# Turning two quarters of the second token group ahead of four products of the first, and pinning four small VectorE operations behind the turned copies

## The chip, the cores and the metric

The kernel runs on one core of a Trainium2 chip. The core has TensorE for matrix products (the profile shows its matmuls as PE and its weight loads as PEld), VectorE (DVE), ScalarE (ACT), GpSimd (POOL) and SyncE (SP), which here issues every DMA. The metric is the device time of one execution in microseconds (us).

## The reference

The input x has 2048 tokens of 448 channels. It is normalised per token (`xn`), and the result is x plus two branches of `xn`:

```python
xn = _layernorm(x, axis=-1)
return x + _A_ref(xn, A_w_r, A_w_i) + _B_ref(xn, B_w1, B_w2, B_w3, B_w4)
# A: real 2-D Fourier transform of xn, times w_r + 1j * w_i, transformed back
# B:
h  = _gelu(_layernorm(x) @ w1)                 # 448 x 448
hs = shifted(h) @ w2                           # each quarter of the channels shifted by +1, -1, +2, -2 tokens
x1 = x + hs
out = x1 + _gelu(_layernorm(x1) @ w3) @ w4     # 448 x 1792 and 1792 x 448
```

The change touches the first part of branch B alone: the product with w1.

## The kernel before

**Tiling.** The tokens lie on 128 partitions as 16 blocks of 128, and the blocks are worked on in four groups of four (`GRP`). Group 0 and group 1 are turned (channels brought to the partitions) on TensorE: `turn_pe(g, t)` writes quarter t of the channels (128 of them, 64 in the last) of all four blocks into one PSUM bank with four transposes (L428). `turn_copy` then makes a high f16 half on ScalarE (L438) and the low half that is left on VectorE (L439). Groups 2 and 3 are turned otherwise: `turn(g)` makes the two halves first (L940 to L942) and sends them block by block through a transposing DMA on SP's queue (L943) into `w4x`, which is the turned input of the products.

**The product with w1.** `w1_in` (L479) multiplies turned blocks with `w1p` in three passes (high by high, low by high, high by low), 44 matmuls of 448 columns for a group. Group 0's four accumulators are `first` (pw1_00 to pw1_03); group 1's are pw1_10 to pw1_13, group 2's pw1_20 to pw1_23. `w1_unit` takes one accumulator further: gelu on ScalarE (L500), a high half (L502) and a low half on VectorE (L503), and a transposing DMA on SP's queue into `h` (L506). The products with w2 (`w2_mm`, L524) read `h`.

**The spreads of the weights.** `powers` forms a power of two for a weight matrix: a sum over partitions by a product with ones (L258, `pm`), then three one-column VectorE operations in `factors`: L265 reads the bank, L267 gives the scale, L270 its inverse. For w2 these are `s2` and `r2`; L1043 to L1045 combine them with w1's into `s12`, which GpSimd reads first at L403.

**What sets the order.** The program is recorded in source order and put in order by a scheduler with its own notion of time; `behind(key)` tells it that what is inside has to stand behind a named instruction, and is no wait on the chip. A row of the orders below with `[waits ...]` waits for a semaphore: each engine counts on one of its own, and a DMA posts on one of eight (DMAHW0 to DMAHW7) taken in turn, after it has itself waited for that semaphore's last user. So the DMAHW name in the row of a DMA is the one that it will post on. Each engine, SP's queue too, works its instructions off strictly in the order in which they stand.

**PSUM banks.** Banks come from pools with two buffers for a name. `pm2`, the bank of the sum for w2, and the last two quarters of group 1 (pta12, pta13) share the two banks called "acc": pta13 takes the bank of `pm2` and has to wait until L265 has read it.

Of the kernel before, what the change touches and what calls it, by code (L numbers as in the profile page):

```python
# [16 lines left out]
ALU = mybir.AluOpType  # L17
# [13 lines left out]
EPS = 1e-5  # L31
# [91 lines left out]
def body(tc, nc, x, wf, w1, w2, w3, w4, c_g, c_n, c_small, out):  # L123
    V, A, P, T, SY = nc.vector, nc.scalar, nc.gpsimd, nc.tensor, nc.sync
# [28 lines left out]
    def bank(tag, name):  # L153
        return ps.tile([128, 512], F32, tag=tag, bufs=2, name=name)
# [10 lines left out]
    def xb(b):  # L165
        g, i = WHERE[b]
        return xt[g][:, i]
# [80 lines left out]
    def powers(m, n, key, tag="acc", mid=None, pin=None, down=0):  # L248

        t = pc.tile([128, 1], F32, name=f"pt{key}")  # L250
        i = V.tensor_reduce(out=t, in_=m[:, :n + 1], axis=AX.X, op=ALU.add)
        after["t" + key] = (i.ins,)
        if mid:
            with behind("t" + key):
                mid()
        pm = bank(tag, f"pm{key}") if isinstance(tag, str) else tag
        with behind(*pin) if pin else contextlib.nullcontext():
            i = T.matmul(pm[:, 0:1], ones, t, start=True, stop=True)  # L258
        after["p" + key] = (i.ins,)
        s, r = factors(pm, key, down)  # L260
        return s, r()

    def factors(pm, key, down=0):
        e = pc.tile([128, 3], I32, name=f"pe{key}")
        V.tensor_scalar(out=e[:, 0:1], in0=pm.bitcast(I32)[:, 0:1], scalar1=1, scalar2=0x7F800000,  # L265
                        op0=ALU.logical_shift_right, op1=ALU.bitwise_and)
        V.tensor_scalar(out=e[:, 1:2], in0=e[:, 0:1], scalar1=-1, scalar2=(185 - down) << 23, op0=ALU.mult, op1=ALU.add)  # L267

        def inverse():
            i = V.tensor_scalar(out=e[:, 2:3], in0=e[:, 0:1], scalar1=1, scalar2=(69 + down) << 23, op0=ALU.mult, op1=ALU.add)  # L270
            after["s" + key] = (i.ins,)
            return e.bitcast(F32)[:, 2:3]

        return e.bitcast(F32)[:, 1:2], inverse
# [61 lines left out]
    def stats1(g, ks):  # L336
        if g not in mvs:
            mvs[g] = pc.tile([128, 4, 2], F32, name=f"mva{GRP[g][0]}")
        stats([xb(GRP[g][k]) for k in ks], f"a{GRP[g][ks[0]]}", mvs[g][:, ks[0]:])
# [70 lines left out]
    after = {}  # L410

    @contextlib.contextmanager
    def behind(*key):
        key = key if len(key) > 1 else key[0]
        with contextlib.ExitStack() as st:
            for i in after[key]:
                st.enter_context(tc.issue_after(i))
            yield
# [4 lines left out]
    def turn_pe(g, t):  # L423
        pt = bank((("mm", "mm", "tr", "tr") if g == 2 else ("tr", "tr", "acc", "acc"))[t], f"pta{g}{t}")
        w = 128 if t < 3 else 64
        with behind("T", g) if ("T", g) in after else contextlib.nullcontext():
            for i, b in enumerate(GRP[g]):
                m = T.transpose(pt[:w, 128 * i:128 * i + 128], xb(b)[:, 128 * t:128 * t + w], ident)  # L428
        after["T", g] = (m.ins,)
        return pt[:w]  # L430
# [42 lines left out]
    def w1_in(g, units, ts, passes=range(3)):  # L473
        for p in passes:
            for t in ts:
                for i, pm in units:
                    wi, xi = ((0, 0), (0, 4), (4, 0))[p]
                    if t < 3 or p != 1:
                        m = T.matmul(pm[:, :D], xTs[g][:, xi + t, 128 * i:128 * i + 128], w1p[:, wi + t],  # L479
                                     start=t == 0 and p == 0, stop=t == 3 and p == 2)  # L480
        return m
# [507 lines left out]
    with behind("p1"):  # L989
        pts = [turn_pe(0, 0)]  # L990
    with behind("T", 0):
        norm_of([3])
    with behind("n", 0):
        s1, r1 = factors(pm, "1")
# [3 lines left out]
    first = [bank("mm" if k < 2 else "sp", f"pw1_0{k}") for k in range(4)]  # L998
# [9 lines left out]
    with behind("w1", -1):  # L1008
        r1 = r1()
    h1 = pc.tile([128, 1], F32, name="h1")  # L1010
# [10 lines left out]
    with behind("n", 1):  # L1021
        pts = [turn_pe(1, t) for t in range(2)]
        with behind("T", 1):
            s2, r2 = powers(m2, 1, "2", "acc", lambda: stats1(2, [0]))
        with behind("p2"):
            after["T", 1] = (w1_in(0, list(enumerate(first)), [3], [2]).ins,)
    with behind("np", 1):
        n1[0][1]()
    with behind("g", 0):
        n1[1][0]()  # L1030
        n1[1][1]()
    pts += [turn_pe(1, 2), turn_pe(1, 3)]
    for t in range(4):
        turn_copy(1, t, pts[t])
    with behind("g", 1):
# [4 lines left out]
        with behind("g", 1):  # L1040
            low()
    s12 = pc.tile([128, 4], F32, name="s12")
    V.tensor_tensor(out=s12[:, 0:1], in0=h1, in1=s2, op=ALU.mult)  # L1043
    V.scalar_tensor_tensor(out=s12[:, 1:2], in0=r1, scalar=2.0 ** 5, in1=r2, op0=ALU.mult, op1=ALU.mult)
    V.tensor_scalar(out=s12[:, 2:3], in0=s12[:, 0:1], scalar1=s12[:, 0:1], scalar2=EPS, op0=ALU.mult, op1=ALU.mult)  # L1045
    p12, eps12 = s12[:, 1:2], s12[:, 2:3]
    stats1(2, [1])
    with behind("a1"):
# [35 lines left out]
    for k in range(4):  # L1084
        n = 128 if k < 3 else 64
        with behind(*((1, 3), (1, 3), (1, 3), (2, 0))[k]):
            squares(m3[:n, k:k + 1], w3raw[:n, k])
    s3, r3 = powers(m3, 4, "3", "sp", pin=("u", 2, 3))
    h3 = pc.tile([128, 1], F32, name="h3")
    V.tensor_scalar(out=h3, in0=s3, scalar1=2.0 ** -6, scalar2=None, op0=ALU.mult)  # L1090
# [23 lines left out]
    for i in range(7):  # L1114
        with behind(3, 3):
            squares(m4[:, i:i + 1], flat(w4raw[:, 2 * i:2 * i + 2]), junk4)
    s4, r4 = powers(m4, 7, "4", down=1)
    p34 = pc.tile([128, 2], F32, name="p34")
    V.scalar_tensor_tensor(out=p34[:, 1:2], in0=r3, scalar=2.0 ** 6, in1=r4, op0=ALU.mult, op1=ALU.mult)
# [122 lines left out]
```

## Time and profile before

| | |
|---|---|
| median of 3 runs | 407.5 us (407.41 to 408.04) |
| the profiled execution, its own time | 407.2 us |
| span of its instructions | 405.4 us |
| TensorE matmul busy | 400.4 us, 99% of the span |
| VectorE, ScalarE, GpSimd busy | 304.4, 267.8, 170.1 us |
| mean granted TensorE clock | 1.0 |

The part that the change touches lies at 19 to 24 us of the span, what it moves farther down at 24 to 60 us; from 60 us on the program consists of the products with w3 and w4 and the Fourier branch. A row of the timeline gives start, length, engine, line, operation, output and inputs, the count of like instructions merged into it, and in brackets the idle time of the engine ahead of it and what ended it. SPq rows are DMAs as SP issues them: the length is that of the issue, not of the transfer.

### The profile page before, as it was taken

How to read it: one execution, taken by the hardware profiler on the slowest of the kernel's cores; microseconds unless marked ns; L12 is line 12 of the kernel's file. 1: busy time of each engine (PE TensorE's matmuls, PEld its weight loads, DVE VectorE, ACT ScalarE, POOL GpSimd, SP SyncE). 2: the span in 40 equal slices, each digit the busy share in tenths (PEclk: the TensorE clock that was granted, in tenths of full speed). 3: DMA queues.
4: the chain of work that ended last, by engine and by line, in shares of the span. 5: the costliest groups of instructions: out<-in, count | busy, mean ns of one | idle time of the engine just before them, and what ended most of it. 6: DMA issues, size and time to landing. Idle time of an engine off the chain costs nothing.

```text
span 405.4 us, 8824 instructions
## 1 busy us (share of the span) xinstructions
PE 400.4 (99%) x3383; PEld 296.6 (73%) x3383; DVE 304.4 (75%) x657; ACT 267.8 (66%) x464; POOL 170.1 (42%) x269
## 2 busy tenths in 40 slices
PE   8999999999999999999999999999999999999996
PEld 4554556666677877776878878877788888888885
DVE  6999999889545658883677777763588879889745
ACT  4699985874738766862687888785956566544332
POOL 2888911001397746599143434431231264211000
PEclk9999999999999999999999999999999999999999
DMA  8999999907910383417054556632000022233201
GB/s 283 340 285 191 175 176 254 267 2 153 211 48 1 100 280 123 115 36 176 15 154 124 144 153 163 156 92 60 1 2 2 24 68 74 89 111 103 84 2 45
DMA packets 57209, 49.46 MB, mean 122 GB/s; under 512 B 41312, under 2 KB 52192, under 8 KB 57168
## 3 DMA queue, kind: packets, MB, share of 16 engines
q1 hardware_dynamic: 57168, 48.91, 46.1%
q8 instruction: 26, 0.43, 0.5%
q14 instruction: 15, 0.12, 0.1%
HBM read 35.06 MB, written 3.67 MB: 96 GB/s over the span
## 4 chain that ended last, share of the span: by engine, by line
PE 99%; DVE 0%; issue 0%
PE pw L449 33%; PE acc L826 24%; PE pw L524 9%; PE pw L479 8%; PE cr L841 4%; PE acc L841 3%; PE pu L722 3%; PE ps L619 3%; PE pp L676 2%; PE pe L742 2%; PE px L693 2%; PE py L764 2%; PE wps L922 2%; PE pta L428 1%; PE end L826 1%; PE pm L985 0%
## 5 line engine op out<-in xcount | busy, mean ns | idle before, releaser
L449 PE MATMUL pw<-x2mem,w3p 128*128 128x256 f16 x1232 | 149.5, 272 | 0.0
L449 PEld LDWEIGHTS <-w3p 128*128 128x128 f16 x1232 | 118.8, 98 | 19.3
L826 PE MATMUL acc<-w4p,hf 128*128 128x448 f16 x508 | 107.3, 352 | 0.0
L826 PEld LDWEIGHTS <-hf 128*128 128x128 f16 x532 | 51.4, 98 | 35.7
L792 DVE SCALAR_TENSOR_TENSOR hf<-pw,h,hf 128x512 f16<-128x512 f32 x56 | 41.8, 747 | 36.0 <-ACT hf L791 35.8
L788 ACT ACTIVATE pw<-pw,pe 128x512 f32<-128x512 f32 x56 | 36.7, 656 | 43.9 <-PE pw L449 43.7
L791 ACT ACTIVATE hf<-pw,h 128x512 f16<-128x512 f32 x56 | 38.3, 683 | 1.2
L524 PE MATMUL pw<-w2p,h 112*128 112x448 f16 x192 | 39.0, 352 | 0.0
L749 POOL TENSOR_TENSOR e<-e 128x226 f32<-128x226 f32 x16 | 10.8, 674 | 64.2 <-ACT e L746 60.9
L479 PE MATMUL pw<-w1p,w4x 128*128 128x448 f16 x176 | 34.8, 352 | 0.5 <-DVE pe L270 0.5
L524 PEld LDWEIGHTS <-h 112*128 112x128 f16 x192 | 18.6, 98 | 16.0 <-DMA h<-x2mem 0.6
L703 POOL TENSOR_TENSOR xr<-te 128x450 f32<-128x450 f32 x16 | 15.7, 982 | 34.1 <-DVE te L701 34.1
L479 PEld LDWEIGHTS <-w4x 128*128 128x128 f16 x176 | 17.1, 98 | 16.4 <-ACT w4x L438 0.7
L711 POOL TENSOR_TENSOR zb<-xr,zb 128x450 f16<-128x450 f32 x16 | 16.2, 1010 | 17.1 <-ACT zb L710 16.5
L756 ACT ACTIVATE vh<-e 128x448 f16<-128x448 f32 x16 | 9.2, 576 | 15.6 <-DVE e L754 15.4
L699 DVE SCALAR_TENSOR_TENSOR te<-px,sc,wc 128x450 f32<-128x450 f32 x16 | 11.0, 686 | 10.3 <-ACT te L698 6.8
L698 ACT ACTIVATE te<-px 64x450 f32<-64x450 f32 x32 | 17.3, 540 | 1.7 <-PE px L693 1.2
L734 ACT ACTIVATE U<-y 113x512 f16<-113x512 f16 x32 | 18.0, 620 | 0.1
L746 ACT ACTIVATE e<-pe 128x452 f32<-128x452 f32 x16 | 8.7, 545 | 13.0 <-PE pe L742 10.1
L726 DVE SCALAR_TENSOR_TENSOR y<-pu,y 113x512 f16<-113x512 f32 x16 | 10.9, 688 | 6.9 <-ACT y L725 6.8
L757 DVE TENSOR_TENSOR vh<-e,vh 128x448 f16<-128x448 f32 x16 | 10.0, 624 | 7.1 <-ACT vh L756 7.1
L598 POOL TENSOR_TENSOR xr<-xf 128x452 f32<-128x452 f32 x6 | 6.7, 1125 | 20.2 <-issue 10.1
(205 smaller groups left out, 786.8 us busy)
## 6 DMA issues: line engine op xcount, KB each, us to landing
wc<-wf SPq DMA_DIRECT2D x32, 225.0 KB, 3.6
wl<-wf SPq DMA_DIRECT2D x8, 450.0 KB, 3.8
xt<-x SPq DMA_DIRECT2D x3, 896.0 KB, 11.6
w3raw<-w SPq DMA_DIRECT2D x3, 896.0 KB, 14.8
xf<-x SPq DMA_DIRECT2D x6, 448.0 KB, 3.7
xr<-x SPq DMA_DIRECT2D x12, 224.0 KB, 2.5
out<-xr SPq DMA_DIRECT2D x12, 224.0 KB, 2.0
gn<-c_g SPq DMA_DIRECT2D x16, 128.0 KB, 3.0
```

Of the source, the lines that this page charges most:

```text
L449: m = T.matmul(ps_out, wp[:, wi + t, cols], xT[:, xi + t, tok], start=t == 0 and wi + xi == 0, stop=t == 3 and wi == 4)
L479: m = T.matmul(pm[:, :D], xTs[g][:, xi + t, 128 * i:128 * i + 128], w1p[:, wi + t], start=t == 0 and p == 0, stop=t == 3 and p == 2)
L524: m = T.matmul(w2b[b][:, :D], hT[g][:112, 4 * hi + k, o:o + 128], w2p[:, wi, k], start=k == 2 and hi + wi == 0, stop=k == 3 and hi == 1)
L698: i = A.activation(out=e[64 * h:64 * h + 64], in_=px_[64 - 64 * h:128 - 64 * h, :2 * DF], func=AF.Copy)
L703: P.tensor_tensor(out=z, in0=t[:, 0], in1=t[:, 1], op=ALU.add)
L711: P.tensor_tensor(out=zv[1], in0=z, in1=zv[0], op=ALU.subtract)
L734: A.activation(out=U[b][:113, p].rearrange("p q (c k) -> p q c k", c=NC), in_=Y1[:113, p, :, :, b], func=AF.Copy)
L788: A.activation(out=pm, in_=pm, func=AF.Gelu_apprx_tanh, scale=r3)
L791: i = A.activation(out=h[:, 0], in_=pv_, func=AF.Copy, scale=h3)
L792: j = V.scalar_tensor_tensor(out=h[:, 1], in0=pv_, scalar=h3, in1=h[:, 0], op0=ALU.mult, op1=ALU.subtract)
L826: m = T.matmul(to, h[:, hi, 2 * f + i], w4p[0][:, wi, 2 * fp + f, r], start=fp == s and f == 0 and hi + wi == 0, stop=fp == e and f == 1 a ...
L841: m = T.matmul(to, h[:, hi, slot] if slot < 4 else g[:, hi, slot - 4], w4f[fp][k][wi], start=k in (0, 6) and fp == 0 and hi == 0, stop=hi ...
```

## The change

Two edits. The first: `turn_pe(1, 2)` and `turn_pe(1, 3)` are recorded where the four products that finish group 0 (quarter 3, third pass, one for each accumulator) were, and these four products behind them. The second: L270 for w2 (`r2`) and the three operations on `s12` are recorded behind the turned copies of group 1 (`behind("a1")`); `powers` returns `r2` uncalled for that.

```diff
-        return s, r()
+        return s, r() if key != "2" else r
...
         with behind("p2"):
-            after["T", 1] = (w1_in(0, list(enumerate(first)), [3], [2]).ins,)
+            pts += [turn_pe(1, t) for t in range(2, 4)]
...
-    pts += [turn_pe(1, 2), turn_pe(1, 3)]
+    with behind("T", 1):
+        w1_in(0, list(enumerate(first)), [3], [2])
     for t in range(4):
         turn_copy(1, t, pts[t])
...
     s12 = pc.tile([128, 4], F32, name="s12")
-    V.tensor_tensor(out=s12[:, 0:1], in0=h1, in1=s2, op=ALU.mult)
-    V.scalar_tensor_tensor(out=s12[:, 1:2], in0=r1, scalar=2.0 ** 5, in1=r2, op0=ALU.mult, op1=ALU.mult)
-    V.tensor_scalar(out=s12[:, 2:3], in0=s12[:, 0:1], scalar1=s12[:, 0:1], scalar2=EPS, op0=ALU.mult, op1=ALU.mult)
+    with behind("a1"):
+        r2 = r2()
+        V.tensor_tensor(out=s12[:, 0:1], in0=h1, in1=s2, op=ALU.mult)
+        V.scalar_tensor_tensor(out=s12[:, 1:2], in0=r1, scalar=2.0 ** 5, in1=r2, op0=ALU.mult, op1=ALU.mult)
+        V.tensor_scalar(out=s12[:, 2:3], in0=s12[:, 0:1], scalar1=s12[:, 0:1], scalar2=EPS, op0=ALU.mult, op1=ALU.mult)
```

The number of instructions on every engine stays the same, and so does every operand. Three places in the order matter.

On TensorE, behind the sum for w2 (pm_350 is `pm2`; pta_355 and pta_371 are quarter 2 of group 1 in the two builds, pta_360 and pta_376 quarter 3; + is the changed kernel):

```order
 L258 MATMUL pm_350<-pt_344,ones 128x1
+L428 MATMUL pta_355<-ident,xt_77 128x128 x4
+L428 MATMUL pta_360<-ident,xt_77 64x128 x4
 L479 LDWEIGHTS w4x
 L479 MATMUL pw_00_219<-w1p,w4x 128x448
@@ -139,6 +141,4 @@
 L479 LDWEIGHTS w4x
 L479 MATMUL pw_03_222<-w1p,w4x 128x448
-L428 MATMUL pta_371<-ident,xt_77 128x128 x4
-L428 MATMUL pta_376<-ident,xt_77 64x128 x4
 L479 LDWEIGHTS w4x
 L479 MATMUL pw_10_447<-w1p,w4x 128x448
```

The eight transposes went ahead of the four products; what stands behind both is group 1's first product, pw_10, as before.

On VectorE, the four low-half copies of group 1 (L439) and the small operations:

```order
 L267 TENSOR_SCALAR pe_352<-pe_352 128x1
+L439 TENSOR_TENSOR w4x<-pta_339,w4x 128x512
+L439 TENSOR_TENSOR w4x<-pta_355,w4x 128x512
+L439 TENSOR_TENSOR w4x<-pta_360,w4x 64x512
 L270 TENSOR_SCALAR pe_352<-pe_352 128x1
-L439 TENSOR_TENSOR w4x<-pta_339,w4x 128x512
-L1043 TENSOR_TENSOR s_397<-h_257,pe_352 128x1
-L1044 SCALAR_TENSOR_TENSOR s_397<-pe_208,pe_352 128x1
-L1045 TENSOR_SCALAR s_397<-s_397 128x1
-L439 TENSOR_TENSOR w4x<-pta_371,w4x 128x512
-L439 TENSOR_TENSOR w4x<-pta_376,w4x 64x512
+L1046 TENSOR_TENSOR s_396<-h_257,pe_352 128x1
```

The copies of quarters 1, 2 and 3 now follow each other, and the small operations stand behind them; L265 and L267 stay ahead.

On SP's queue, farther down, the four transposing DMAs that turn group 2 (L943, one for each of its blocks; the scheduler has moved these by itself):

```order
 L506 DMA_TRANSPOSE h_446<-hs_119 128x8x128 [waits DMAHW4_49,DVE_49]
 L943 DMA_TRANSPOSE w4x<-x_463 128x7x128 [waits DVE_49,DMAHW5_49,PE_49,Activation_49]
-L943 DMA_TRANSPOSE w4x<-x_463 128x7x128 [waits DMAHW6_49,PE_49]
+L943 DMA_TRANSPOSE w4x<-x_463 128x7x128 [waits DMAHW6_49,DVE_49,Activation_49]
 L943 DMA_TRANSPOSE w4x<-x_463 128x7x128 [waits DVE_49,DMAHW7_49,PE_49,Activation_49]
 L943 DMA_TRANSPOSE w4x<-x_463 128x7x128 [waits DMAHW0_49,PE_49]
```

The row of the first DMA reads the same in both builds, but it now carries block 1 of the group, and the second, which has got waits for its own data, carries block 0. What TensorE waits for shows it. Ahead of the first product of group 2 (pw_20, block 0) TensorE stood before:

```order
L524 MATMUL pw_1_532<-w2p,h_446 128x448
L524 LDWEIGHTS h_446
L524 MATMUL pw_1_532<-w2p,h_446 128x448
L479 LDWEIGHTS w4x [waits DMAHW5_49]
L479 MATMUL pw_20_631<-w1p,w4x 128x448 [waits DVE_49]
```

and in the changed kernel:

```order
L524 MATMUL pw_1_532<-w2p,h_446 128x448
L524 LDWEIGHTS h_446
L524 MATMUL pw_1_532<-w2p,h_446 128x448
L479 LDWEIGHTS w4x [waits DMAHW6_49]
L479 MATMUL pw_20_631<-w1p,w4x 128x448 [waits DVE_49]
```

The weight load of block 0 waited for the first of the four DMAs (DMAHW5), and now waits for the second (DMAHW6), while the place of the product in TensorE's order has not moved. Later on SP's queue the last L943 of group 3 and one L506 of group 2 have changed places as well.

## The prediction

> **What bounds the kernel now.** I read the page's busy times and its chain of waits first, then what TensorE waited for, then the timeline of the stretch that the change touches, and last the queue of SP behind it.
>
> ```profile
> PE 400.4 (99%) x3383; PEld 296.6 (73%) x3383; DVE 304.4 (75%) x657; ACT 267.8 (66%) x464; POOL 170.1 (42%) x269
> ...
> PE 99%; DVE 0%; issue 0%
> ```
>
> The whole chain that ends last is TensorE's own queue. What TensorE waited for, with total, times and longest:
>
> ```profile
> PE wps L922 <- DVE x2mem L188: 1.2, 1, 1.2
> PE pw L479 <- DVE pe L270: 0.5, 1, 0.5
> ```
>
> Both waits lie at the start, ahead of the change. So the kernel has no slack on TensorE: the change removes no matmul, hence it can gain only what small gaps TensorE still has behind 19 us, and any new wait of TensorE goes into the time in full. A matmul's record is longer than its step, so gaps below some 0.16 us do not show as idle time; I get them from counts. The timeline:
>
> ```profile
> 12.39 6.97 PE L479 MATMUL pw<-w1p,w4x 128*128 128x448 f16 x36
> ...
> 19.84 1.09 ACT L438 ACTIVATE w4x<-pta 128x512 f16<-128x512 f32 x2 [1.69 <-PE pta L428]
> ...
> 20.08 0.28 PE L258 MATMUL pm<-pt,ones 128*128 128x1 f32 x2
> ...
> 20.22 0.92 PE L479 MATMUL pw<-w1p,w4x 128*128 128x448 f16 x4
> ...
> 20.40 0.16 DVE L265 TENSOR_SCALAR pe<-pm 128x1 int32<-128x1 int32 x1 [0.73 <-PE pm L258]
> ...
> 20.98 1.04 PE L428 MATMUL pta<-ident,xt 128*128 128x128 f32 x8
> ...
> 21.20 0.68 DVE L439 TENSOR_TENSOR w4x<-pta,w4x 128x512 f16<-128x512 f32 x1
> ...
> 21.61 1.07 ACT L438 ACTIVATE w4x<-pta 128x512 f16<-128x512 f32 x2 [0.68 <-PE pta L428]
> ...
> 21.80 0.15 DVE L1043 TENSOR_TENSOR s<-h,pe 128x1 f32<-128x1 f32 x1
> ...
> 21.85 8.65 PE L479 MATMUL pw<-w1p,w4x 128*128 128x448 f16 x44
> ...
> 22.24 1.41 DVE L439 TENSOR_TENSOR w4x<-pta,w4x 128x512 f16<-128x512 f32 x2
> 22.58 0.59 ACT L500 ACTIVATE pw<-pw,gsc 128x448 f32<-128x448 f32 x1
> 23.21 0.63 ACT L502 ACTIVATE hs<-pw,h 128x448 f16<-128x448 f32 x1
> ...
> 23.70 6.36 PEld L479 LDWEIGHTS <-w4x 128*128 128x128 f16 x35 [0.43 <-DVE w4x L439]
> ...
> 23.87 0.68 DVE L503 SCALAR_TENSOR_TENSOR hs<-pw,h,hs 128x448 f16<-128x448 f32 x1 [0.23 <-ACT hs L502]
> ```
>
> The step of a 448-column product is (6.97 - 0.35) / 35 = 0.189 us (0.35 is one record). At 23.70 a weight load of group 1 waited for the copy of the last quarter, which ended at 22.24 + 1.41 = 23.65. How much of that reached the products:
>
> ```profile
> 30.34 7.09 PE L524 MATMUL pw<-w2p,h 112*128 112x448 f16 x36
> 37.27 7.92 PE L479 MATMUL pw<-w1p,w4x 128*128 128x448 f16 x41
> ```
>
> 44 products from 21.85 to 30.34 took 8.49 us where 44 x 0.189 is 8.32: a gap of 0.17. 36 products from 30.34 to 37.27 took 6.93 where 36 x 0.189 is 6.80: 0.13 more. These 0.3 us are all that the change can win between 19 and 37 us.
>
> **The front of the change.** The eight transposes start at 20.22 and not at 20.98, 0.76 earlier. They take 21.85 - 20.98 = 0.87, so the four products run from 21.09 and group 1 starts at 21.85 as before: the swap itself costs TensorE nothing. ScalarE's copy of quarter 2 was released at 21.61; it now could start at 20.85 but ScalarE copies quarters 0 and 1 until 19.84 + 1.09 = 20.93, so the gain is about 0.7, and gelu goes from 22.58 to about 21.85. VectorE lost 22.24 - 21.80 = 0.44 to the small operations between its copies; with these behind, quarters 1, 2 and 3 follow each other from 21.15 and end near 23.15 instead of 23.65. The weight load that waited at 23.70 wanted to go at 23.70 - 0.43 = 23.27, so the 0.17 goes.
>
> The bank of `pm2`: quarter 3's first transpose comes four steps of 0.11 (0.87 / 8) after 20.22, at 20.66, and needs L265, which ended at 20.56. That is 0.10 ahead, and holds, since L265 still stands ahead of the copies; if it failed the price would be under 0.1. Cost 0. `s12` ends later by about 1.2 us; it is read first here:
>
> ```profile
> 36.10 0.57 POOL L403 TENSOR_SCALAR cs<-cs,s 128x4 f32<-128x4 f32 x2
> ```
>
> With 13 us to spare these four operations cost nothing, and L270's result goes into `s12` alone.
>
> **What it triggers on SP's queue.** The first transposing DMA waits for L503 at 23.87, which now follows gelu and L502 0.75 earlier. So SP starts its chain at up to 24.64 - 0.75 = 23.89. Each row: start, length of the issue.
>
> ```profile
> 24.64 1.66 SPq L506 DMA_TRANSPOSE h<-hs  x1
> ...
> 26.41 1.96 SPq L506 DMA_TRANSPOSE h<-hs  x1
> ...
> 28.48 1.25 SPq L506 DMA_TRANSPOSE h<-hs  x1
> ...
> 29.83 2.65 SPq L506 DMA_TRANSPOSE h<-x2mem  x2
> 32.57 1.29 SPq L506 DMA_TRANSPOSE h<-hs  x1
> 34.03 5.29 SPq L943 DMA_TRANSPOSE w4x<-x  x4
> ...
> 35.34 1.25 SPq L943 DMA_TRANSPOSE w4x<-x  x1
> ```
>
> Each issue starts some 0.1 to 0.2 us behind the end of the one before: from 24.64 on SP itself is the limit, eight issues long, down to the second L943. And there TensorE stands close behind:
>
> ```profile
> 34.98 2.01 PEld L524 LDWEIGHTS <-h 112*128 112x128 f16 x12 [0.38 <-DMA h<-x2mem]
> 37.15 2.87 PEld L479 LDWEIGHTS <-w4x 128*128 128x128 f16 x16 [0.16 <-DMA w4x<-x]
> ```
>
> The time from issue to landing stands last in the row of a DMA:
>
> ```profile
> w4x<-x SPq DMA_TRANSPOSE x1, 3.1
> ```
>
> The first L943 (34.03, landing 3.1 later at 37.13) was block 0 of group 2, and the weight load at 37.15 took it at once; the product followed at 37.27. In the changed order block 0 rides in the second L943: issued at 35.34, 3.1 to land (its row reads the same), so 38.44 - x, where x is how much earlier SP's chain comes to that place. With the 0.02 to 0.05 from landing to weight load the product starts at 38.49 - x instead of 37.27: **TensorE ends up 1.22 - x later than before**. The 0.3 won ahead of it is in that already, since it only makes TensorE wait longer here.
>
> **How large x is.** Its ends are 0, if the earlier start is eaten up by longer issues, and 0.75, if every issue keeps its length. The two first issues are the long ones, 1.66 and 1.96 against 1.25 to 1.29, 1.1 us more in all. The stretches, with the DMA engines' share and GB/s last:
>
> ```profile
> 22.00:24.00 2.00, 2.00 (x12) 0.89 (x10) 1.70 (x5) 1.97 (x5) 2.00 (x5) 1.00 1.00 419
> 24.00:26.00 2.00, 2.00 (x13) 0.99 (x12) 1.82 (x4) 2.00 (x5) 1.92 (x4) 1.00 1.15 291
> 26.00:28.00 2.00, 2.00 (x12) 1.06 (x11) 1.79 (x5) 2.00 (x5) 1.79 (x2) 1.00 1.25 127
> ```
>
> Up to 24 us the engines are full with the loads of x and w3; when the transposes come in, the rate falls and the share stays above 1. A transpose issued 0.75 earlier meets 0.75 x 419 = 315 KB more of loads, and that has to be moved at the slow rate, with the issues stretched for longer. So x lies nearer to 0 than to 0.75; I take 0.3, and TensorE is 1.22 - 0.3 = 0.9 us late from 37 us on. That is an estimate from these rows. The first of them took this long to land, where the L943 took 3.1:
>
> ```profile
> h<-hs SPq DMA_TRANSPOSE x1, 5.3
> ```
>
> The Trainium skill, page "DMA: Bandwidth & Descriptors", section "Queues, rings and completion order", says that on each DMA engine descriptors are consumed in ring order; all of this kernel's DMAs stand in SP's row of rings, so by it alone the transposes cannot pass the loads, x would be close to 0 and the loss 1.2 us. The trace agrees in part, with 5.3 us against 3.1; it does not tell how much of the issue time goes with it.
>
> Nothing behind 37 us can give the loss back, since TensorE has no idle time there. The sum for the profiled execution: 407.2 + 0.9 = 408.1. The runs' median is 0.3 above that execution, so 407.5 + 0.9 = **408.4 us**.
>
> **The rivals.** *A second wait.* The other swap on SP's queue puts a transpose of `h` (group 2) behind the last L943 of group 3:
>
> ```profile
> 50.53 1.25 SPq L506 DMA_TRANSPOSE h<-x2mem  x1
> 51.94 1.22 SPq L943 DMA_TRANSPOSE w4x<-x  x1
> ...
> 54.25 0.48 PEld L524 LDWEIGHTS <-h 112*128 112x128 f16 x3
> ```
>
> and the landing of the first of these rows:
>
> ```profile
> h<-x2mem SPq DMA_TRANSPOSE x1, 3.2
> ```
>
> It would be issued at about 51.9, land 3.2 later at 55.1, and be wanted at 54.25 + 0.9 = 55.15. If SP's queue is late there by as much as TensorE, it costs up to 0.85 more: 409.2 us. Against it: the group 3 halves ahead of it on that queue don't wait for TensorE's late products, and the changed order puts two more products ahead of the one that wants it (0.4 us).
>
> *No wait at all, and the time not slower.* If the first two issues fall back to 1.25 because the loads are done with, x is 0.75 + 1.1 = 1.85, the second L943 lands at 36.6, ahead of 36.97 where TensorE would want it, and the 0.3 stays: 407.2 us. The point from which it decides is x = 1.22. The 419 GB/s of loads right before 24 us speak against it.
>
> *The full shift.* x = 0.75: 0.47 late, 408.0 us; this is the low end of my own case, as x = 0 (408.7) is its high end.
>
> *The change does nothing.* The swap of blocks 0 and 1 would have to be harmless because TensorE comes to group 2 later anyhow; but every product between 20 and 37 us stands where it stood, and only gaps have gone. 407.5 us.
>
> **How the numbers follow.** 0.2% of 407.5 is 0.8 us, about what a measurement of this kernel can tell from no change. My case (408.0 to 408.7) gets 0.76: 0.27 of it below 408.3, 0.49 above. The second wait gets 0.08, no wait, or a change that does nothing, 0.11, time lost at a place that I don't see 0.03, and won there 0.02. So slower by over 0.2%: 0.49 + 0.08 + 0.03 = 0.60; within 0.2%: 0.27 + 0.11 = 0.38; faster: 0.02. The range runs from 407.6, between no wait and the full shift, to 409.0, short of the second wait's end.
>
> **What the profile of the changed kernel would show.** TensorE's waits: a new line for L479 waiting for the DMA of `w4x`, 0.6 to 1.2 us, at 37 us, and the row of 41 products there starting near 38.2; no wait of a weight load for L439 at 23.7; gelu L500 near 21.9, and SP's first transpose near 23.9. If the first two issues are again 1.7 to 2.0 long and the third starts later than 27.7, x was eaten as I say. I am wrong if the second L943 is issued ahead of 34.1, if TensorE shows no wait at 37 us, or if its order lets it do other work there.

## The result and the profile after

The changed kernel takes 408.72 us (median of 15 runs, 407.83 to 409.71), the kernel before 407.5 us in the same comparison (407.28 to 408.41). The ratio is 1.002, with a 95% interval of 1.0011 to 1.0029: slower by 0.45 to 1.2 us. The profiled execution took 407.97 us with a span of 406.2 us, so it lies near the fast end of its own kernel; the median is 0.75 us longer.

The page of the changed kernel, busy times and chain:

```profile
PE 399.8 (98%) x3383; PEld 296.7 (73%) x3383; DVE 304.6 (75%) x657; ACT 268.0 (66%) x464; POOL 171.9 (42%) x269
...
PE 93%; DVE 3%; ACT 2%; DMA 1%; issue 0%; DVEq 0%; ACTq 0%
```

TensorE is busy for 0.6 us less (99% to 98%) in a span that is 0.8 us longer: it waits more. What TensorE waited for (total, times, longest):

```profile
PE wps L922 <- DVE x2mem L188: 1.2, 1, 1.2
PE pw L479 <- DVE xt L531: 0.8, 1, 0.8
PE pm L985 <- ACT xr L246: 0.6, 2, 0.3
PE pw L479 <- DVE pe L270: 0.5, 1, 0.5
```

The second row is new, and stands ahead of group 2's first product; the third is new too, but lies near 7 us, ahead of the change. The second names VectorE, since L531 happened to end at 38.01 in this execution, and the chain follows it there (DVE 3%, ACT 2%); the weight load of that product names a DMA instead, and so do the rows of the same wait in all later profiles. The timeline of the changed kernel, TensorE's queue and the copies:

```profile
21.21 9.24 PE L479 MATMUL pw<-w1p,w4x 128*128 128x448 f16 x48
21.22 2.00 DVE L439 TENSOR_TENSOR w4x<-pta,w4x 128x512 f16<-128x512 f32 x3
21.95 0.59 ACT L500 ACTIVATE pw<-pw,gsc 128x448 f32<-128x448 f32 x1
...
23.39 0.68 DVE L503 SCALAR_TENSOR_TENSOR hs<-pw,h,hs 128x448 f16<-128x448 f32 x1
...
30.29 6.97 PE L524 MATMUL pw<-w2p,h 112*128 112x448 f16 x36
...
38.02 2.00 PEld L479 LDWEIGHTS <-w4x 128*128 128x128 f16 x12 [1.19 <-DMA w4x<-x]
38.02 8.50 PE L479 MATMUL pw<-w1p,w4x 128*128 128x448 f16 x44 [0.75 <-DVE xt L531]
```

The 48 products from 21.21 run without a gap (the weight load's wait at 23.7 is gone), gelu begins at 21.95 instead of 22.58, and then group 2's first product starts at 38.02 instead of 37.27: 0.75 later. SP's queue in the same execution (start, length of the issue):

```profile
24.14 1.34 SPq L506 DMA_TRANSPOSE h<-hs  x1
...
25.64 2.23 SPq L506 DMA_TRANSPOSE h<-hs  x1
...
27.97 1.28 SPq L506 DMA_TRANSPOSE h<-hs  x1
...
33.54 1.24 SPq L943 DMA_TRANSPOSE w4x<-x  x1
```

The first transposing issue is 0.50 earlier, the second 0.77 (it is then held longer), and from the third down to the first L943 (34.03 before) everything is 0.5 earlier. Group 2's first product comes 38.02 - 33.54 = 4.48 behind that issue: one more issue and 3.1 us of landing.

### The profile page after: what moved, and what is told of

Same layout as the page of the kernel before. It is cut to its first block, busy times and chain, and to the rows that moved or that the text cites. A ratio compares the mean times of both kernels' runs of the same rounds, so it can differ in the third digit from the quotient of the medians.

```text
span 406.2 us, 8827 instructions
## 1 busy us (share of the span) xinstructions
PE 399.8 (98%) x3383; PEld 296.7 (73%) x3383; DVE 304.6 (75%) x657; ACT 268.0 (66%) x464; POOL 171.9 (42%) x269
## 4 chain that ended last, share of the span: by engine, by line
PE 93%; DVE 3%; ACT 2%; DMA 1%; issue 0%; DVEq 0%; ACTq 0%
PE pw L449 33%; PE acc L826 24%; PE pw L524 7%; PE pw L479 6%; PE cr L841 4%; PE acc L841 3%; PE pu L722 3%; PE ps L619 3%; PE pp L676 2%; PE pe L742 2%; PE px L693 2%; PE py L764 2%; DVE sta L326 1%; DMA xt<-x 1%; ACT pw L500 1%; PE pta L428 1%
## 5 line engine op out<-in xcount | busy, mean ns | idle before, releaser
L479 PE MATMUL pw<-w1p,w4x 128*128 128x448 f16 x176 | 34.4, 352 | 1.3 <-DVE xt L531 0.8
L479 PEld LDWEIGHTS <-w4x 128*128 128x128 f16 x176 | 17.1, 98 | 17.3 <-DMA w4x<-x 1.2
L711 POOL TENSOR_TENSOR zb<-xr,zb 128x450 f16<-128x450 f32 x16 | 16.1, 1009 | 17.1 <-ACT zb L710 16.5
```

The lines of the kernel that those rows point to most:

```text
L711: P.tensor_tensor(out=zv[1], in0=z, in1=zv[0], op=ALU.subtract)
```

## Experiments

Two times are used in all of them, both counted from the same instruction, the start of the pm matmul L258 near 20 us, so that what happens ahead of the change (19.89 to 20.70 us) drops out. The table is worked out from the rows of each timeline; the landing of the last w3 load is its issue (L219) plus the time from issue to landing in its row. "Product" is group 2's first L479 behind the 36 products of w2.

| kernel | L258 at | last w3 load lands at | third L506 issue at | first L943 issue, from L258 | product, from L258 |
|---|---|---|---|---|---|
| before | 20.08 | 28.62 | 28.48 | 13.95 | 17.19 |
| before, second profile | 20.46 | 29.65 | 29.59 | 14.69 | 18.07 |
| before, third profile | 20.01 | 28.09 | 28.46 | 14.02 | 17.35 |
| changed | 20.16 | 28.06 | 27.97 | 13.38 | 17.86 |
| changed, second profile | 20.22 | 29.12 | 29.04 | 14.38 | 18.84 |
| changed, third profile | 20.12 | 28.34 | 28.30 | 13.74 | 18.36 |
| changed, block 0 first | 20.35 | 28.26 | 28.25 | 13.44 | 16.94 |
| before, swap alone | 20.34 | 28.15 | 28.10 | 13.46 | 17.99 |
| before, turn alone | 20.70 | 28.65 | 28.66 | 13.53 | 18.11 |
| before, pinned alone | 19.89 | 28.20 | 28.16 | 13.83 | 17.19 |
| changed, both orders back | 20.10 | 28.80 | 28.74 | 14.18 | 17.55 |
| changed, no late loads | 19.94 | none | 26.78 | 12.95 | 17.45 |
| before, no late loads | 20.43 | none | 27.88 | 13.44 | 17.07 |

**Block 0 first.** The changed kernel; each L943 of group 2 is ordered behind the one of the block ahead of it:

```diff
-            d = SY.dma_start_transpose(out=xTs[g][:, :, 128 * i:128 * i + 128], in_=h)
+            with behind("td", g, i - 1) if g == 2 and i else contextlib.nullcontext():
+                d = SY.dma_start_transpose(out=xTs[g][:, :, 128 * i:128 * i + 128], in_=h)
+            after["td", g, i] = (d.ins,)
```

> The changed kernel, with the four L943 transposes of group 2 held in the order of their blocks, so that block 0 goes first again. Theory (the loss is block 0 riding in the second L943): the 0.75 us step of TensorE at 37 us and its weight load's 1.2 us wait are gone; the first L943 is issued near 33.5 and lands near 36.6, ahead of the 36.97 at which TensorE wants it, so the 0.3 us won ahead of it stay: 407.2 us, ratio to the kernel before 0.9993, and slower than before by nothing. Rival (the loss lies in the turned quarters or the small operations themselves): the step at 37 us goes but 0.5 us or more turn up elsewhere, 408 us or more, ratio above 1.001. Rival (second wait): as TensorE is on time again, the transpose of h that stands behind the last L943 of group 3 is now late at 54 us by 0.1 to 0.5 us: 407.3 to 407.7.

Measured: 408.17 us, ratio 1.001 (1.0001 to 1.0018). The step at 37 us is gone, the product comes 0.25 earlier than in the first profile of before; but at 54 us a new wait stands. TensorE in this kernel:

```profile
37.29 8.49 PE L479 MATMUL pw<-w1p,w4x 128*128 128x448 f16 x44
...
55.27 0.74 PE L524 MATMUL pw<-w2p,h 112*128 112x448 f16 x3 [0.27 <-DMA h<-x2mem]
```

From start to start the gap there is 0.43 above the step. So block 0's place is what costs time at 37 us, and the order holds a second loss in reserve, which shows only when TensorE is on time: 0.43 - 0.25 = 0.18 late in the profile, within the interval (0.04 to 0.73 us). The 407.2 of the theory failed. The second wait came as its rival said (0.1 to 0.5 us), but the median lies above that rival's 407.7 and inside the range of the other one (408 or more); the profiled execution is the fastest of its eleven. What speaks for the second wait is the trace, in which nothing else is lost behind the product (see the two kernels again, below).

**Swap alone.** The kernel before; block 1's L943 of group 2 goes ahead of block 0's, and nothing else is changed:

```diff
+            def send(i=i, h=h):
+                with behind("td", 2, 1) if g == 2 and i == 0 else contextlib.nullcontext():
+                    d = SY.dma_start_transpose(out=xTs[g][:, :, 128 * i:128 * i + 128], in_=h)
...
+        for i in (1, 0, 2, 3) if g == 2 else range(4):
+            d = sends[i]()
```

> The kernel before with one edit: block 1's L943 of group 2 is sent ahead of block 0's; nothing else of the change. Theory: SP's chain starts at 24.64 as before, so x is 0 and TensorE is 1.22 us late at 37 us: 408.7 us, ratio 1.0030, with a weight load of L479 waiting for the DMA of w4x there. Rival (the order of the two blocks doesn't matter, the loss is elsewhere): 407.5 us, ratio 1.000, no step at 37 us.

Measured: 408.69 us, ratio 1.0027 (1.0019 to 1.0036). This one edit gives the whole loss. TensorE and SP:

```profile
38.33 8.50 PE L479 MATMUL pw<-w1p,w4x 128*128 128x448 f16 x44 [0.75 <-DMA w4x<-x]
```

```profile
24.90 1.34 SPq L506 DMA_TRANSPOSE h<-hs  x1
...
33.80 1.23 SPq L945 DMA_TRANSPOSE w4x<-x  x1
```

Yet x was not 0. The first issue stood where it stood before (24.90 - 20.34 = 4.56 from L258, as 24.64 - 20.08), and the first L943 still came 0.49 earlier. So the 0.5 us of the changed kernel's profile need not come from its earlier first issue, and the median met the expected 408.7 without the x of 0 from which that was reckoned.

**Turn alone.** The kernel before with the turned quarters moved; the small operations stay:

```diff
-            after["T", 1] = (w1_in(0, list(enumerate(first)), [3], [2]).ins,)
+            pts += [turn_pe(1, t) for t in range(2, 4)]
...
-    pts += [turn_pe(1, 2), turn_pe(1, 3)]
+    with behind("T", 1):
+        w1_in(0, list(enumerate(first)), [3], [2])
```

> The kernel before with only the turned quarters ahead of the four products; the four small VectorE operations stay where they were, between the copies of quarters. Theory: it is this half that swaps blocks 0 and 1 on SP's queue, so TensorE is late at 37 us, by 1.22 - x. The copies end about 0.4 us later than in the changed kernel, but they do not lead to SP's first transpose, which waits for L503 alone; L503 itself no longer has two small operations ahead of it (0.1 to 0.15 us), so x is 0.5 to 0.65 and the step 0.6 to 0.75: 408.1 to 408.3 us, ratio 1.0015 to 1.002. Rival (the pinned operations make the loss): 407.3 us, ratio 0.9995, no step at 37 us.

Measured: 408.88 us (five runs), ratio 1.0035 (1.0021 to 1.0049). That is more than the 408.1 to 408.3 expected; whether it is more than the whole change costs can't be told, since the intervals overlap. Weight load waits of this kernel:

```profile
19.77 0.86 PEld L428 LDWEIGHTS pta<-ident,xt 128*128 128x128 f32 x8 [0.50 <-POOL xt L370]
...
21.94 4.07 PEld L479 LDWEIGHTS <-w4x 128*128 128x128 f16 x22
...
38.81 1.25 PEld L479 LDWEIGHTS <-w4x 128*128 128x128 f16 x8 [1.44 <-DMA w4x<-x]
```

This half of the change alone swaps the blocks and makes the loss; it also alone removes the wait at 23.7 (22 loads in a row). The 0.50 at 19.77 lies ahead of the moved instructions and cost this execution 0.22; it is not in the column "from L258". In that column the product is 0.92 later than in the first profile of before (18.11 against 17.19), where 0.6 to 0.75 was expected, since the first L943 came only 0.42 earlier.

**Pinned alone.** The kernel before with only the four small operations pinned:

```diff
-        return s, r()
+        return s, r() if key != "2" else r
...
+    with behind("a1"):
+        r2 = r2()
+        V.tensor_tensor(out=s12[:, 0:1], in0=h1, in1=s2, op=ALU.mult)
```

> The kernel before with only the four small VectorE operations pinned behind the copies. Theory: SP's order stays that of before, the copy of the last quarter ends up to 0.44 us earlier, the weight load's wait at 23.70 and the 0.17 us behind it go: 407.3 us, ratio 0.9996, at most no change. Rival (the pinned operations make the loss): 408.2 us or more, ratio 1.002.

Measured: 407.79 us, ratio 0.9998 (0.9989 to 1.0007): no change. VectorE and the weight load:

```profile
22.05 1.41 DVE L439 TENSOR_TENSOR w4x<-pta,w4x 128x512 f16<-128x512 f32 x2 [0.42 <-ACT w4x L438]
...
24.09 0.68 DVE L503 SCALAR_TENSOR_TENSOR hs<-pw,h,hs 128x448 f16<-128x448 f32 x1
```

```profile
23.51 2.57 PEld L479 LDWEIGHTS <-w4x 128*128 128x128 f16 x15 [0.43 <-DVE w4x L439]
```

With the small operations out of the way VectorE idles instead, since the copies of quarters 2 and 3 need ScalarE's copy first (0.42). The weight load waits for 0.43 as before: that this wait would go was wrong. In return L503 starts at 24.09, while its input (L502) ended at 23.64.

**Both orders back.** The block-0-first kernel with the rest of SP's order put back too:

```diff
-            with behind("td", g, i - 1) if g == 2 and i else contextlib.nullcontext():
+            with behind("td", g, i - 1) if g == 2 and i else behind("h", 2, 1) if g == 3 and i == 3 else contextlib.nullcontext():
...
+            with behind("h", 2, 3) if b < 2 else contextlib.nullcontext():
```

> The changed kernel with SP's whole order put back to that of before: group 2's L943 transposes in the order of their blocks, and the last L943 of group 3 behind the second transpose of h for group 2. Theory (the change moves TensorE's time only through these two places on SP's queue): against the block-0-first kernel the wait of 0.27 us at 55.27 goes, no step at 37 us, and the time from quarter 0's turn on is 0.25 to 0.3 us below that of before: 407.2 to 407.3 us, ratio 0.9993. Rival (the turned quarters or the pinned operations cost time of their own): 407.8 us or more, ratio 1.0008 or more.

Measured: 407.96 us, ratio 1.0008 (0.9996 to 1.002). The theory's 0.9993 lies just outside that interval, the rival's 1.0008 is what was measured, and no change at all is not excluded. TensorE and SP:

```profile
31.25 6.57 PE L524 MATMUL pw<-w2p,h 112*128 112x448 f16 x33 [0.29 <-DMA h<-hs]
...
52.36 1.87 PE L479 MATMUL pw<-w1p,w4x 128*128 128x448 f16 x9
54.40 0.74 PE L524 MATMUL pw<-w2p,h 112*128 112x448 f16 x3 [0.17 <-DMA h<-x2mem]
```

```profile
25.58 3.06 SPq L506 DMA_TRANSPOSE h<-hs  x1
```

Two things. In this execution the second issue was held for 3.06 us, and the w2 products came to the transposes of group 0's h too early (from start to start 0.45 and 0.15 lost): what TensorE wins in front it waits for there. And the wait at 54 us is still there with SP's order back, 0.33 from start to start: TensorE's own order now asks for that h behind 9 products, where before it was 13. The theory that these two places on SP's queue are all fell as far as the second is concerned. The rival is not shown by it either: this one execution lost in the w2 products and at 54 us, in both places waiting for a transpose of h.

**The loads.** Over the table one thing stands out: in ten of the eleven profiles that have these loads, the third transposing issue starts within 0.15 us of the landing of the last w3 load, at whatever time that is, and the first L943 follows it. (In pinned alone, one of the ten, the second issue was short, and the match may be chance.) The rows from which the landing is read, here for the first profile of the changed kernel (the issue, and the time from issue to landing):

```profile
11.56 0.47 SPq L219 DMA_DIRECT2D w3raw<-w  x1
```

```profile
w3raw<-w SPq DMA_DIRECT2D x1, 448.0 KB, 16.5
```

11.56 + 16.5 = 28.06, against 27.97 for the third issue. To test it, the loads of w3's last two row blocks were left out of the changed kernel and of the kernel before:

```diff
-    load_w3([2, 3])
+    P.memset(w3raw[:, 2], 2.0 ** -6); P.memset(w3raw[0:64, 3], 2.0 ** -6)
```

> The changed kernel without the loads of w3's last two row blocks (the tile is filled with a constant, so the output is not the reference's); the other loads are then done some 3.2 us earlier (1344 KB at 420 GB/s), near 24.3. Theory L (the second transposing issue is held until the last load packet has ended, and the third starts 0.45 us behind that): the first two issues are near 1.3 us each, the third starts near 27.0 instead of 27.97, the second L943 lands a full 1.0 us earlier, and the wait of TensorE at 37 us (0.75) goes: 407.2 us, ratio 0.9993. Rival S (the length of SP's chain doesn't hang on the loads, only on its start): third issue at 27.9, step at 37 us still 0.6 to 0.8, 408.2 us.

> The kernel before with the same loads left out as in the changed kernel without late loads (w3's last two row blocks are a constant, the output is not the reference's). Theory L (SP's chain follows the end of the loads): the first three issues are 1.25 to 1.35 each, the third starts near 27.5 instead of 28.48, the first L943 lands before TensorE wants it, the gap of 0.13 in the w2 products goes, and group 2's first product comes 17.05 us behind the pm matmul of L258 at 20 us, against 17.45 in the changed kernel without these loads: there the change costs 0.4 us, and the time here is 407.4 us, ratio 0.9997. Rival (the order of the two blocks costs its full 1.22 us when no load disturbs): 16.2 to 16.3 would be needed, which TensorE's own work doesn't allow.

Measured: changed 407.85 us, ratio 1.0006 (0.9998 to 1.0015); before 407.55 us, ratio 1.0001 (0.9992 to 1.001). SP in the changed kernel without these loads, and TensorE:

```profile
23.93 1.34 SPq L506 DMA_TRANSPOSE h<-hs  x1
...
26.78 1.27 SPq L506 DMA_TRANSPOSE h<-hs  x1
28.16 1.28 SPq L506 DMA_TRANSPOSE h<-x2mem  x1
...
30.10 1.23 SPq L506 DMA_TRANSPOSE h<-x2mem  x1
```

```profile
37.39 2.57 PEld L479 LDWEIGHTS <-w4x 128*128 128x128 f16 x15 [0.78 <-DMA w4x<-x]
```

The loads do hold the second issue: without them it is done by 26.7, and the third starts at 26.78. Counted from L258 that is 0.97 earlier than in the first profile of the changed kernel (6.84 against 7.81), as theory L had it (27.0 for 27.97). But the gain does not reach the L943: behind 28.16 + 1.28 = 29.44 SP waits for data, the first block of group 1, as its waits in this stretch tell:

```profile
SPq L506 <- DVE x2mem L503: 0.6, 1, 0.6
```

So the first L943 is only 0.43 earlier from L258, and TensorE still waits (0.78 by the weight load above). With the loads away, the change costs 17.45 - 17.07 = 0.38 us at the product, in one profile of each; by the two ratios it is 0.2 us, and their intervals overlap. That the wait would vanish was wrong. For the kernel before, the product came as expected (17.07 against 17.05), the third issue later (27.88 against 27.5), and the gap in the w2 products is gone. Without the loads the earlier first issue (0.58) does reach the chain in these two profiles: the third issue is 0.61 and the first L943 0.49 ahead of those of the kernel before.

The last w3 load (L219) is a slow one: 64 rows of 7168 bytes, 448 KB. In each of the eleven profiles the last 64 packets of this size, as many as the load has rows, take 483 to 646 ns each on average, and the 64 ahead of them 272 to 276; without the late loads they take some 272 ns to the end. From the start of the first of those 64 to the end of the last it takes 3.1 to 4.4 us, which is 105 to 147 GB/s, where 416 to 441 GB/s were moved from 22 to 24 us. It is not the transposes that begin this: in five profiles the load is slow ahead of the first of them. Here is pinned alone, its first transposing issue, and then three stretches with the engines' busy times, and last the DMA engines' share and GB/s:

```profile
24.85 1.86 SPq L506 DMA_TRANSPOSE h<-hs  x1
```

```profile
22.00:24.00 2.00, 2.00 (x12) 0.89 (x10) 1.89 (x6) 1.97 (x5) 2.00 (x5) 1.00 1.04 437
24.45:24.80 0.35, 0.35 (x3) 0.20 (x2) 0.35 (x2) 0.35 (x2) 0.27 (x2) 1.00 1.23 211
24.85:26.00 1.15, 1.15 (x8) 0.60 (x7) 1.12 (x3) 1.15 (x3) 1.15 (x3) 1.00 1.06 162
```

Why this load is slow, and how much the transposes then add, no run here tests.

**The two kernels again.** Unchanged, for how far such a profile can be trusted:

> The changed kernel once more, unchanged, for how much its places move from run to run. Theory L: whatever the end of the last load packet is (27.5 to 28.1 so far), the third transposing issue starts 0.44 to 0.50 us behind it, and TensorE's step at 37 us follows with the same shift, 0.6 to 1.0 us. Theory E (the earlier start of the first issue sets it): third issue 0.5 us ahead of that of before in every run, step 0.75.

> The kernel before once more, unchanged. Theory L: third issue 0.44 to 0.50 us behind the end of the last load packet; its place may differ by some tenths from the 28.48 of the first profile, with no step at 37 us above 0.15. Theory E: third issue at 28.5 again, as the first issue again starts near 24.6 to 24.9.

> The changed kernel, unchanged, a third profile. Theory L: the end of the last w3 load lies anywhere from 27.5 to 29.2, the third transposing issue within 0.15 us of its landing, and group 2's first product 4.45 us behind the first L943 issue (1.3 to the second, 3.1 to land, 0.05), whatever the time.

> The kernel before, unchanged, a third profile. Theory L: the same for the third transposing issue; where the last load lands later than 28.7, the w2 products wait for the DMA of h for 0.3 to 1.0 us, and where it lands earlier they don't.

They took 409.01 and 408.44 us (changed), 408.45 and 407.3 us (before). The second profile of the changed kernel, SP and TensorE:

```profile
25.69 3.24 SPq L506 DMA_TRANSPOSE h<-hs  x1
```

```profile
31.56 6.57 PE L524 MATMUL pw<-w2p,h 112*128 112x448 f16 x33 [0.48 <-DMA h<-hs]
39.06 8.50 PE L479 MATMUL pw<-w1p,w4x 128*128 128x448 f16 x44 [0.94 <-DMA w4x<-x]
```

The same of the kernel before, its second profile:

```profile
27.00 2.49 SPq L506 DMA_TRANSPOSE h<-hs  x1
```

```profile
31.06 7.63 PE L524 MATMUL pw<-w2p,h 112*128 112x448 f16 x36 [0.18 <-DMA h<-hs]
```

And of the third profile of the kernel before, SP:

```profile
24.57 2.44 SPq L506 DMA_TRANSPOSE h<-hs  x1
...
27.12 1.23 SPq L506 DMA_TRANSPOSE h<-hs  x1
28.46 1.28 SPq L506 DMA_TRANSPOSE h<-hs  x1
```

So the place of SP's chain moves by 0.74 (before) and 1.00 (changed) between executions of one kernel, and group 2's first product moves with it in both: in the late ones even the kernel before waits, in its w2 products. Theory E fell: the third issue of before was at 28.46 to 29.59. Theory L held but for the third profile of before, where the first issue was the long one (2.44), the second was short, and the third started 0.37 behind the landing. That profile's w2 products lost 0.26 us from start to start, those of the second profile, where the last load landed at 29.65, lost 0.95: as expected, the late landing is what makes them wait.

In all six profiles with block 1 first, the product comes 4.46 to 4.62 behind the first L943's issue: the loss at 37 us has no other part. Over the three profiles of each kernel the first L943 comes at 14.22 (before) and 13.83 (changed) from L258, the product at 17.54 and 18.35: 0.81 us, where the ratio of the times says 0.82. With places that move by 0.7 to 1.0, that the two agree so closely is chance.

What is left behind the product is the same in all. The time of the profiled execution (407.2, 408.45 and 407.3 for before, 407.97, 409.01 and 408.44 for the changed kernel, 408.27, 408.77 and 407.05 for the swap, the turn and the pinned operations alone), less the place of the product, is 369.92 to 369.97 us in all nine. It is 0.1 more in the two kernels without the late loads, and 0.43 and 0.35 more in block 0 first (407.66) and both orders back (407.94), which is their wait at 54 us. So the changed kernel loses nothing behind group 2's first product, and its three profiled executions differ only by when that product starts.

## Why the prediction was right, and where not

**TensorE is the bound, with 0.3 us to win.** Right. With block 0 first the product came 0.25 earlier than in the first profile of before, and no kernel here was measurably faster than before. But the 0.3 was read off an early execution: against the mean of the three profiles of before (17.54) those 16.94 are 0.60 earlier.

**The swap costs TensorE nothing, and the wait at 23.7 goes.** Right, 48 products in a row, and the bank of `pm2` held nothing up: the eight transposes run from 20.30 and the first product behind them starts at 21.21, 0.91 later (0.87 before). But the text gave it to both halves of the change; the runs give it to the turned quarters alone. The pinned operations alone won nothing, since VectorE then waited for ScalarE's copy.

**The small operations cost nothing.** Right in the time (0.9998). The step missed that two of them now stand ahead of L503 (23.25 to 23.39 in the changed kernel), so SP's first issue came 0.58 earlier from L258 and not 0.75.

**TensorE ends up 1.22 - x later.** Right: the first profile has 1.22 - 0.50 = 0.72 by the clock of the trace and 0.75 at the product; the swap alone gives the loss, and putting block 0 back takes it away.

**How large x is.** The size was near: 0.39 as the mean of three profiles against three, where 0.3 was taken, and 408.4 was forecast where 408.72 was measured. The reason was not right, so that the size came out near is in part luck. The step let x follow from the earlier first issue, between 0 and 0.75. With the loads in place, the chain follows the end of the loads instead: x against the first profile of before was 0.57, -0.43 and 0.21 in three executions of the changed kernel, and 0.49 in a kernel whose first issue had not moved. The landing of the last load lies 8.26 us behind L258 on average in the six profiles with the early turn and these loads, and 8.39 in the five without: a difference of 0.13 with a spread of over 1. Whether the earlier start moves the chain at all beside the loads stays open. That the start was "eaten up" was the right picture: the long second issue ends with the loads. But the rate does not fall because the transposes come in, as the step read its three stretches: it falls with the last w3 load, in five profiles before any transpose is issued. So it does not follow that a transpose issued earlier has 315 KB more moved at the slow rate.

**The rule of ring order** ("DMA: Bandwidth & Descriptors", section "Queues, rings and completion order", in the Trainium skill) gave x near 0 and a loss of 1.2. The trace agrees in that in nine of the eleven profiles the second transposing issue ends just behind the last packet of the loads ahead of it. It doesn't show that no transpose passes a load: in the first profile of the changed kernel the first packets of 256 bytes, which appear only behind the first transposing issue, start at 25.93, and the last load packet ends at 27.52. Which packets share an engine it doesn't tell, nor whether it is the ring or the shared engines that hold the issue, as no run here used a second ring.

**The rivals.** The second wait did not come in the changed kernel in three profiles; it came with 0.43 as soon as TensorE was on time, so "if SP's queue is late there by as much as TensorE" was the right condition. Of its reason only half held: with both orders back the wait was still there, as TensorE asks for that h earlier in that kernel. "No wait at all" needed x = 1.22; even with the loads gone x reached 1.0 from L258 (13.95 - 12.95), because SP then waits for group 1's first block. "The full shift" is what the first profile happens to show, within 0.2.

**The range.** The median was expected 0.3 above the profiled execution; that was taken from before, and for the changed kernel it is 0.75. The prediction read one execution as the kernel's own timing, where a chain of DMAs moves by 0.7 to 1.0 us from one execution to the next. Of its signs, the wait at 37 us came (0.75, the product at 38.02) and the third issue was later than 27.7 (27.97); the two first issues were not both long (1.34 and 2.23).

Open: whether the changed order with both places on SP's queue put back is faster or slower than before (0.9996 to 1.002), and what makes the loads end at times up to 1.4 us apart, counted from L258, in executions of much the same work: the last w3 load itself takes 3.1 to 4.4 us, and starts 3.8 to 4.5 behind L258.

## What to carry to other kernels

When the order of work on one engine is changed, read what a scheduler does with the DMA queue behind it: here the moved matmuls cost nothing, and two transposes that changed places on SP's queue made the whole loss. Ask for each DMA which consumer comes first, and keep them in that order. A wait that is covered by another shows only when the first is repaired, and a time that hangs on the end of large loads is to be read from several executions, not from one.

## What was not expected of the hardware

A DMA transpose that SP issues beside large loads can hold SP's queue until the loads are done. In nine of the eleven profiles with these loads the second issue was lengthened, to 1.54 to 3.24 us, where it took 1.23 and 1.26 in the two kernels without them, and it ended 0.32 to 0.42 us behind the last packet of the loads. In the other two (pinned alone, and the third profile of before) the first issue was held instead, for 1.86 and 2.44, and the second was short (1.23 in both); the first was long in the first two profiles of before as well (1.66 and 1.86), and 1.34 everywhere else. The packets of the last load (7168 bytes) took longer themselves: by the trace's records of packets in the first profile of the changed kernel (means over those that started in the stretch), 272 ns each between 23 and 24 us, 577 ns between 25 and 26. As pinned alone shows, that begins without any transpose. From the L943's issue to its landing it took 3.0 to 3.4 us for the four blocks of group 2 in all of these kernels, whatever the loads did ahead of it.
